# Second layer of the expert pairs with the tokens as columns, turned back by DMA, in a Mamba-2 and top-1 routing kernel

## The chip, the core and the metric

The kernel runs on one core of a Trainium2 chip. A core has engines that run their own instruction streams and wait for each other on semaphores: TensorE (PE, matrix multiplies, with weight loads PEld beside them), VectorE (DVE), ScalarE (ACT), GpSimd (POOL) and SyncE (SP, which issues DMA transfers here). The metric is the device time of one execution in microseconds (us), the median of several runs.

## What is computed

Two stages follow each other. The first is a state-space layer (chunks of a scan over 768 places, 4 batches, 8 heads of 32); it yields x, 3072 tokens of 256 numbers. The second, which the change concerns, sends each token to one of 8 experts:

```python
logits = x @ w_gate                      # 3072 x 8
expert_idx = np.argmax(logits, axis=1)
probs = np.exp(logits - logits.max(-1, keepdims=True))
probs /= probs.sum(-1, keepdims=True) + 1e-09
gate_w = probs[np.arange(N), expert_idx]
for e in range(E):                       # E = 8
    mask = expert_idx == e
    h = np.maximum(x[mask] @ w1[e], 0.0)         # 256 -> 1024
    out[mask] = gate_w[mask, None] * (h @ w2[e]) # 1024 -> 256
```

How many tokens an expert gets is known only while the kernel runs.

## The kernel before

**Places and passes.** Each expert has a stretch of rows in the DRAM buffer `x_hbm`; a token's row holds its 256 numbers, its 8 logits and its number. GpSimd's indirect DMAs scatter the tokens there (`place`, L553). A first pass handles the first 256 places (CA) of every expert, expert by expert; a second pass handles the next 192 places (CB), two experts at a time, as pairs v = 0 to 3; a general loop after that is for inputs with more tokens yet (L983). Rows with no token carry a number out of bounds, so that their output is dropped.

**One expert.** A tile `xs` holds rows with tokens as partitions. The first layer needs x with its 256 numbers as partitions: `halves` (L645) splits the fp32 words into 16-bit halves on VectorE (L651), a DMA transposes the 128x128 blocks (L653), and `words` (L657) joins the halves to `xT`. `m_h` (L692) runs the first layer: for each of the 8 blocks of 128 hidden units, two matmuls with a 128x128 block of w1 loaded and n columns of `xT` streaming, into one of four PSUM banks (`h_ps`, L681), then a relu on ScalarE into `hT` (L696), with hidden units as partitions and tokens as columns. `m_y` (L717) runs the second layer with 128 tokens of `hT` as the loaded side and the 256 columns of w2 streaming, so the result has tokens as partitions; `put` multiplies by the gate, a number per partition, and `send` (L708) scatters the rows to `out`. The profile shows every fp32 matmul as two records.

**The second pass** (L962 to L980). Of a pair, 128 places of each expert lie in `xs[:, 0]` and `xs[:, 1]`, the last 64 of each share a tile `xh`. The number of columns of `m_h` is chosen at run time: `over` (L567) makes for each pair a class from its greater expert's count, and `tc.Switch` (L966) jumps to one of five cases, with widths of 128, 144, 160, 176 and 192. Only TensorE and ScalarE enter the cases (`pairs_on`, L896); the other engines jump past. A case holds both experts' `m_h` and, from the second case on, `m_half` (L726): the second layer of the last 64 places of both experts, side by side in the array, scaled by the gate into `yh`. After the case come `send(yh)`, the hint that tells the sequencers of TensorE and ScalarE which case is next (`switch_hint`, L974), and for the next pair the joining of words (`b_words`), the gates (`b_gates`: VectorE and ScalarE's Exp) and the transpose of the pair after it (`next_halves`). The second layer of the 128 first places, `m_y` for both experts, stands last, after the switch (L979).

**Order.** All of it stands under `tc.manual_schedule()` (L779): each engine executes its own instructions in the order in which the program writes them. Where a tile name has n buffers (`bufs=n`), the n+1st tile of that name takes the first one's place and waits for its readers. `hT` has three buffers, `xT` three, `pl` and `plT` two each. Memsets on VectorE (L965) clear `hT` from column 144 on before each pair, for columns that a case does not write but `m_half` reads.

The transfers of the second pass are the pairs' rows (L606 and L609), the transposes, both on SyncE's queue, and the scatters on GpSimd's.

Of the kernel before, what the change touches and what calls it, by code (L numbers as in the profile page):

```python
# [9 lines left out]
FP32 = mybir.dt.float32  # L10
BF16 = mybir.dt.bfloat16
I32 = mybir.dt.int32
U16 = mybir.dt.uint16
AX = mybir.AxisListType.X
ALU = mybir.AluOpType
# [5 lines left out]
N, DM, E, F = 3072, 256, 8, 1024  # L21
# [14 lines left out]
CA, CB = 256, 192  # L36
CAP = CA + CB
TA = CA // 128
NK = -(-(N - CAP) // 128)
NR = N + 128  # L40
EW = 2


@with_exitstack
def ssd_then_moe(ctx, tc, x, ad_in, az_in, B, BT, CT, w_gate, w1, w2, out):
# [521 lines left out]
    def over(tb, pp):  # L567
        cp = pp.tile([128, RG + 1, E], FP32, name="cn", tag="rank", bufs=1)
        nc.tensor.matmul(cp[:, 0], lhsT=ones_bf, rhs=cnt[:, len(RGS) + 1, :], start=True, stop=True)
        cn = tb.tile([128, E], FP32, name="cn")  # L570
        nc.vector.tensor_tensor(out=cn, in0=cp[:, 0], in1=base2, op=ALU.add)
        nc.vector.tensor_tensor(out=cn, in0=cn, in1=base_f, op=ALU.subtract)
        ov = tb.tile([128, E], FP32, name="ov")
        nc.vector.tensor_scalar(out=ov, in0=cn, scalar1=float(127 - CAP), scalar2=0.0, op0=ALU.add, op1=ALU.max)
        nc.vector.tensor_copy(nk[:, 0:E], ov)
        nc.vector.tensor_scalar(out=nk[:, 0:E], in0=nk[:, 0:E], scalar1=7, scalar2=None, op0=ALU.logical_shift_right)
        fl = tb.tile([128, 2], FP32, name="fl")
        nc.vector.tensor_reduce(fl[:, 0:1], ov, axis=AX, op=ALU.max)
        nc.vector.tensor_scalar(out=nk[:, E:E + 1], in0=fl[:, 0:1], scalar1=127.0, scalar2=None, op0=ALU.is_gt)
        nc.vector.tensor_copy(nk[:, E + 1:2 * E + 1], cn)  # L580

        ml = tb.tile([128, E // 2], FP32, name="ml")
        nc.vector.tensor_reduce(ml, cn.rearrange("p (b i) -> p b i", i=2), axis=AX, op=ALU.max)
        nc.vector.tensor_scalar(out=ml, in0=ml, scalar1=float(15 - CA - 128), scalar2=0.0, op0=ALU.add, op1=ALU.max)
        nc.vector.tensor_scalar(out=ml, in0=ml, scalar1=64.0, scalar2=None, op0=ALU.min)
        cl = nk[:, 2 * E + 1:]
        nc.vector.tensor_copy(cl, ml)
        nc.vector.tensor_scalar(out=cl, in0=cl, scalar1=4, scalar2=None, op0=ALU.logical_shift_right)


    ex = [dict() for _ in range(E)]
# [28 lines left out]

    def gate_out(sub, n):
        nc.scalar.activation(sub, sub, func=ACT.Exp)
        gt = ea.tile([128, TA], FP32, name="gate", bufs=5)[:, 0:n]
        nc.vector.tensor_reduce(gt, sub, axis=AX, op=ALU.add)
        nc.vector.tensor_scalar(out=gt, in0=gt, scalar1=1e-9, scalar2=None, op0=ALU.add)
        nc.vector.reciprocal(gt, gt)
        return gt
# [5 lines left out]
        return p  # L633

    def new_xT():
        return ea.tile([128, KT, CA], FP32, name="xT", bufs=3)

    def a_xT(e, pp, tag):
        ex[e]["xT"] = new_xT()
# [49 lines left out]
    def new_hT(mo):  # L689
        return mo.tile([128, FT, CA], FP32, name="hT", bufs=3)  # L690

    def m_h(e, xT, hT, n, pp, between=None):  # L692
        for f in range(FT):

            p = up(xT[:, :, 0:n], w_sb[e][0], f, n, pp, 128 if e == f == 0 and n == CA else CA)
            nc.scalar.activation(hT[:, f, 0:n], p, func=ACT.Relu)  # L696
            if between and f == FT // 2:
                between()

    def put(p, xs, gt, mo, scalar=True, last=False):  # L700
        yo = mo.tile([128, DM], FP32, name="yo", bufs=3)
        if scalar:
            nc.scalar.mul(yo, p, gt)  # L703
        else:
            nc.vector.tensor_scalar(out=yo, in0=p, scalar1=gt, scalar2=None, op0=ALU.mult)  # L705
        send(yo, xs, last)
# [8 lines left out]
        tc.add_to_no_dep_group("sc", s_.ins)  # L715

    def m_y(e, hT, xs, gt, mo, pp, between=None, scalar=True, last=False):  # L717
        p = pp.tile([128, DM], FP32, name="y_ps", tag="y", bufs=2)
        for f in range(FT):
            nc.tensor.matmul(p, lhsT=hT[:, f], rhs=w_sb[e][1][:, f * DM:f * DM + DM], start=(f == 0),  # L720
                             stop=(f == FT - 1))
            if between and f == FT // 2:
                between()
        put(p, xs, gt, mo, scalar, last)

    def m_half(v, mo, pp):  # L726

        p = pp.tile([128, DM], FP32, name="yh_ps", tag="rank", bufs=1)
        for f in range(FT):
            for i in range(2):  # L730
                nc.tensor.matmul(p[64 * i:64 * i + 64, :], lhsT=pr[v]["hT"][i][:, f, 128:CB],  # L731
                                 rhs=w_sb[2 * v + i][1][:, f * DM:f * DM + DM], start=(f == 0), stop=(f == FT - 1))
        nc.scalar.mul(yh, p, pr[v]["gh"])  # L733
# [45 lines left out]
    with tc.manual_schedule():  # L779
# [118 lines left out]
        def ab(e, t):  # L898
            def then():

                if e >= 1 and late:
                    place(late.pop(0))
                if e == E - 1 and t == 0:
                    b_words(0)
                if 2 <= e < 2 + E // 2 and t == 1:
                    v = e - 2
                    r = nc.values_load(nk[0:1, 2 * E + 1 + v:2 * E + 2 + v], engines=pairs_on, min_val=0, max_val=4,
                                       skip_runtime_bounds_check_because="one of five classes")
                    cls.append({g: r for g in pairs_on})
            return then  # L910
        def b_gates(v):
            r = pr[v]
            r["gate"] = gate_out(gate_in(r["xs"], TA), TA)
            r["gh"] = gate_out(gate_in(r["xh"], 1), 1)
        for e in range(E + 1):
            def nxt():
                if e == 0:
                    ex[0]["sub"] = gate_in(ex[0]["xs"], TA)
                    empty(2)
                    empty(3)  # L920
                    a_load(2)
                    a_load(3)
                    load_w(2, (0,))
                if e == 1:
                    rank_pe(last, rank_ps)
                    rank(last)
                if e == 2:
                    over(tb, pp)
                if e + 1 < E:
                    a_words(e + 1)  # L930
                    ex[e + 1]["sub"] = gate_in(ex[e + 1]["xs"], TA)
                next_halves(e + 2)
                if 1 <= e and e + 2 < E:
                    load_w(e + 2)
                if e == 0:
                    load_w(1, (1,))
                    load_w(2, (1,))
                    empty(4)
                    empty(5)
                if e == 1:  # L940
                    empty(6)
                    empty(7)
            if e < E:
                ex[e]["hT"] = new_hT(mo)
                m_h(e, ex[e]["xT"], ex[e]["hT"], CA, pp, nxt)
                ex[e]["gate"] = gate_out(ex[e]["sub"], TA)
                if e == E - 1:
                    b_gates(0)
            if e == E:
                tc.switch_hint(cls[0], 5, "p0")  # L950
            if e > 0:
                for t in range(TA):
                    m_y(e - 1, ex[e - 1]["hT"][:, :, 128 * t:128 * t + 128], ex[e - 1]["xs"][:, t],
                        ex[e - 1]["gate"][:, t:t + 1], mo, pp, ab(e - 1, t), e < E)
                if e + 3 < E:
                    a_load(e + 3)
                elif e + 3 - E < E // 2:
                    b_load(e + 3 - E, mo)

        yh = mo.tile([128, DM], FP32, name="yh", bufs=1)  # L960
        nc.vector.memset(yh, 0.0)
        for v in range(E // 2):  # L962
            pr[v]["hT"] = [new_hT(mo) for _ in range(2)]
            for h in pr[v]["hT"]:
                nc.vector.memset(h[:, :, 144:CB], 0.0)  # L965
            for c in tc.Switch(cls[v], 5, f"p{v}"):  # L966
                for i in range(2):
                    m_h(2 * v + i, pr[v]["xT"][i], pr[v]["hT"][i], 128 + 16 * c, pp)
                if c:
                    m_half(v, mo, pp)  # L970

            send(yh, pr[v]["xh"][:, 0])
            if v + 1 < E // 2:
                tc.switch_hint(cls[v + 1], 5, f"p{v + 1}")  # L974
                b_words(v + 1)
                b_gates(v + 1)
                next_halves(E + v + 2)
            for i in range(2):
                m_y(2 * v + i, pr[v]["hT"][i][:, :, 0:128], pr[v]["xs"][:, i],  # L979
                    pr[v]["gate"][:, i:i + 1], mo, pp, None, False, (v, i) == (E // 2 - 1, 1))  # L980
        mo_.close()
    more = nc.values_load(nk[0:1, E:E + 1], min_val=0, max_val=1, skip_runtime_bounds_check_because="a truth value")
    with tc.If(more > 0):  # L983
# [49 lines left out]
```

## Time and profile before

| | |
|---|---|
| median of three runs | 271.99 us (271.18 to 272.0) |
| span in the profile | 270.0 us |
| granted TensorE clock | 0.992 of full speed |
| busy: PEld, DVE, ACT, POOL | 213.7, 110.7, 104.5, 87.0 us |
| second pass, first to last matmul | 194.56 to 262.8 us |
| first-layer records L685, all forms | 90.3 us in 516 records |
| second-layer records L720 | 84.9 us in 384 records |
| half tiles L731 | 7.3 us in 64 records |

A line of a group view names the source line, engine and operation, the tiles (output <- inputs), shapes and count, then busy time and mean length. [...] records start closer together than they are long, so the time that they take is read from the starts of the first and last. In timelines each line has start, length, what, and in brackets how long the engine was idle before it and what it waited for. Names ending in q are sequencers: branches and register moves, which count as no engine's busy time.

### The profile page before, as it was taken

What the parts mean: (1) busy time and instruction counts of PE and PEld (TensorE: products, weight loads), DVE (VectorE), ACT (ScalarE), POOL (GpSimd) and SP (SyncE); (2) the same over time, 40 slices, a digit from 0 to 9 for tenths busy, and PEclk for the clock granted to TensorE, in tenths of its full rate; (3) what the DMA queues carried; (4) which work ended last, traced back from release to release, by engine and by line L of the source; (5) the groups of instructions that cost most, each with busy time, mean ns of one, the idle gap of its engine ahead of it and who ended that gap; (6) DMA issues with size and microseconds to landing.
All of it is one profiled execution on the core that took longest, in us unless ns stands there. A gap on an engine that the chain in (4) does not pass through costs nothing.

```text
span 270.0 us, 7603 instructions
## 1 busy us (share of the span) xinstructions
PE 252.9 (94%) x3044; PEld 213.7 (79%) x3067; DVE 110.7 (41%) x358; ACT 104.5 (39%) x304; POOL 87.0 (32%) x171
## 2 busy tenths in 40 slices
PE   8799898999997999999999999999999999999990
PEld 2577677677776888888888888888998978989770
DVE  4889887888854240421211111233225115321010
ACT  6958574655543423223232323141050520604200
POOL 5666875866720002025504120202211102121021
PEclk9999999999999999999999999999999999999996
DMA  6956767671434899949695959533330601401010
GB/s 182 374 172 171 228 199 236 165 247 51 135 118 101 212 367 310 384 177 294 236 256 202 279 199 335 130 91 78 103 85 9 94 4 30 90 6 40 2 35 28
DMA packets 29715, 43.57 MB, mean 161 GB/s; under 512 B 16203, under 2 KB 19917, under 8 KB 27984
## 3 DMA queue, kind: packets, MB, share of 16 engines
q1 hardware_dynamic: 27152, 36.32, 45.4%
q0 software_dynamic: 2496, 6.41, 7.1%
q8 instruction: 36, 0.59, 0.9%
q14 instruction: 31, 0.25, 0.3%
HBM read 29.10 MB, written 10.73 MB: 147 GB/s over the span
## 4 chain that ended last, share of the span: by engine, by line
PE 82%; DVE 5%; DMA 4%; issue 4%; POOL 2%; ACT 1%; POOLq 0%; ACTq 0%; DVEq 0%
PE h_ps L685 33%; PE y_ps L720 30%; PE y L176 5%; PE rows_ps L176 4%; PE g L176 3%; PE A L176 3%; PE yh_ps L731 3%; DVE L L359 2%; DMA x_hbm<-rows,pos 1%; DMA xs<-x_hbm 1%; DMA az<-in_az_dram 1%; DMA ct<-in_CT_dram 1%; DVE M L386 1%; PE rank L176 1%; DVE S L431 1%
## 5 line engine op out<-in xcount | busy, mean ns | idle before, releaser
L685 PE MATMUL h_ps<-xT,w 128*128 128x256 f32 (+3 forms) x516 | 90.3, 334 | 0.6 <-ACT xT L641 0.5
L685 PEld LDWEIGHTS h_ps<-xT,w 128*128 128x128 f32 x516 | 81.3, 190 | 8.2 <-ACT xT L641 0.7
L720 PE MATMUL y_ps<-w,hT 128*128 128x256 f32 x384 | 84.9, 380 | 0.0
L720 PEld LDWEIGHTS y_ps<-w,hT 128*128 128x128 f32 x384 | 72.6, 190 | 10.5 <-issue 0.8
L696 ACT ACTIVATE hT<-h_ps 128x256 f32<-128x256 f32 (+3 forms) x128 | 43.3, 339 | 60.8 <-PE h_ps L685 53.1
L711 POOL DMA_INDIRECT out_dram<-yo,xs x24 | 23.7, 988 | 91.1 <-ACT yo L703 64.7
L553 POOL DMA_INDIRECT x_hbm<-rows,pos x24 | 24.4, 1015 | 20.6 <-DMA x_hbm<-zrows 13.3
L359 DVE TENSOR_TENSOR_SCAN L<-abc,ident 128x512 f32<-128x512 f32 x24 | 29.1, 1213 | 0.0
L651 DVE COPY pl<-xs 128x256 uint16<-128x256 uint16 x44 | 10.4, 298 | 43.8 <-DMA xs<-x_hbm 43.7
L658 DVE COPY xT<-plT 128x512 uint16<-128x512 uint16 (+1 forms) x30 | 10.6, 415 | 33.6 <-DMA plT<-pl 27.8
L703 ACT ACTIVATE yo<-y_ps,gate 128x256 f32<-128x256 f32 x14 | 6.6, 474 | 39.4 <-PE y_ps L720 24.5
L386 DVE TENSOR_TENSOR M<-g,L 128x512 f32<-128x512 f32 x24 | 16.5, 687 | 5.6 <-PE g L176 5.1
L176 PE MATMUL rows_ps<-turn,yT 128*128 128x136 f32 x96 | 15.4, 283 | 3.5 <-issue 2.7
L705 DVE TENSOR_SCALAR yo<-y_ps,gate 128x256 f32<-128x256 f32 x10 | 4.8, 482 | 29.3 <-PE y_ps L720 29.3
L176 PE MATMUL g<-ctm,bt 32*64 32x128 f32 x384 | 16.3, 280 | 0.5 <-ACT ctm L293 0.4
L176 PEld LDWEIGHTS rows_ps<-turn,yT 128*128 128x128 f32 x96 | 14.5, 192 | 1.3 <-issue 0.4
L711 POOL DMA_INDIRECT out_dram<-yh,xh x4 | 3.9, 978 | 35.7 <-ACT yh L733 23.9
L470 ACT COPY rows<-rows_ps 128x264 f32<-128x264 f32 x24 | 9.1, 380 | 13.5 <-PE rows_ps L176 10.9
L176 PE MATMUL y<-M,xn 64*32 64x64 f32 x768 | 12.9, 223 | 1.2 <-issue 1.2
L457 ACT COPY yT<-y 128x256 f32<-128x256 f32 x24 | 8.9, 372 | 12.2 <-PE y L176 10.2
L176 PEld LDWEIGHTS g<-ctm,bt 32*64 32x64 f32 x384 | 10.4, 131 | 3.2 <-ACT ctm L293 0.9
L366 POOL TENSOR_TENSOR bs<-bn,L 128x128 f32<-128x128 f32 x22 | 9.0, 410 | 11.1 <-DVE L L359 10.0
(132 smaller groups left out, 203.3 us busy)
## 6 DMA issues: line engine op xcount, KB each, us to landing
w<-in_w_dram SPq DMA_DIRECT2D x13, 1024.0 KB
x_hbm<-zrows SPq DMA_DIRECT2D x8, 463.8 KB
xn<-in_x_dram SPq DMA_DIRECT2D x12, 256.0 KB
w<-in_w_dram SPq DMA_DIRECT2D x12, 256.0 KB
xs<-x_hbm SPq DMA_DIRECT2D x8, 265.0 KB
ct<-in_CT_dram SPq DMA_DIRECT2D x6, 256.0 KB
bt<-in_BT_dram SPq DMA_DIRECT2D x6, 256.0 KB
bn<-in_B_dram SPq DMA_DIRECT2D x6, 256.0 KB
```

The costliest lines, as they stand in the source:

```text
L176: i = nc.tensor.matmul(out, lhsT=lhsT, rhs=rhs, **kw)
L359: nc.vector.tensor_tensor_scan(out=s["L"].rearrange("p h i -> p (h i)"), data0=s["abc"], data1=ident8.rearrange("p h i -> p (h i)"), initi ...
L366: nc.gpsimd.tensor_tensor(out=bs[n % 2], in0=gr[n // CG]["B"][:, n % CG].rearrange("p (h m) -> p h m", h=8), in1=bc(st[n]["L"][:, :, CH - ...
L386: nc.vector.tensor_tensor(out=s["M"].rearrange("p (s v u) i -> p s v (u i)", s=2, v=2), in0=s["g"][:, :, 0:256].rearrange("p v (s f) -> p ...
L470: nc.scalar.copy(out=rt[g][:, k - R0[g], 0:DM + E], in_=p)
L553: s_ = nc.gpsimd.indirect_dma_start(out=x_hbm[:, :], out_offset=bass.IndirectOffsetOnAxis(ap=pos[:, k:k + 1], axis=0), in_=rt[grp[k]][:, k ...
L651: nc.vector.tensor_copy(pl[:, i, :, t], f[:, :, HB * t:HB * t + 128])
L658: nc.vector.tensor_copy(xT.bitcast(U16).rearrange("p t (j c) -> p c t j", c=2), tt)
L685: nc.tensor.matmul(p[:, i:min(i + step, n)], lhsT=w[:, c:c + 128], rhs=xT[:, t, i:min(i + step, n)], start=(t == 0), stop=(t == KT - 1))
L696: nc.scalar.activation(hT[:, f, 0:n], p, func=ACT.Relu)
L711: s_ = nc.gpsimd.indirect_dma_start(out=out[:, :], out_offset=bass.IndirectOffsetOnAxis(ap=xs[:, TOK:TOK + 1].bitcast(I32), axis=0), in_=y ...
L720: nc.tensor.matmul(p, lhsT=hT[:, f], rhs=w_sb[e][1][:, f * DM:f * DM + DM], start=(f == 0), stop=(f == FT - 1))
```

## The change

For pairs 0 to 2 the second layer is computed with its tokens as columns. `m_yT` loads 128x128 blocks of w2 and streams as many columns of `hT` as the first layer has made, for both experts inside the switch's case; the result, with the 256 outputs as partitions, is copied by ScalarE to `yT`. After the case `turn_back` splits it into 16-bit halves, a DMA transposes them as it does for the inputs, and `put_back` joins the words, multiplies by the gates on VectorE and sends three tiles. The second layer then streams only as many columns as there are places, in place of 256 for each tile, and `m_half` is not needed. Since columns may now be any number, the classes are 8 places apart from 112 to 192: eleven cases. Pair 3 keeps the old second layer. The next pair's words are joined ahead of the switch, and the gates are made one pair earlier (pairs 0 and 1 both behind expert 7); `xT` and `yo` get four buffers and the gates eight. The memsets of `hT` remain for pair 3 alone, from column 112.

```diff
+NCL = 11
-        nc.vector.tensor_scalar(out=ml, in0=ml, scalar1=float(15 - CA - 128), scalar2=0.0, op0=ALU.add, op1=ALU.max)
-        nc.vector.tensor_scalar(out=ml, in0=ml, scalar1=64.0, scalar2=None, op0=ALU.min)
+        nc.vector.tensor_scalar(out=ml, in0=ml, scalar1=float(7 - CA - 112), scalar2=0.0, op0=ALU.add, op1=ALU.max)
+        nc.vector.tensor_scalar(out=ml, in0=ml, scalar1=float(8 * NCL - 8), scalar2=None, op0=ALU.min)
...
-        nc.vector.tensor_scalar(out=cl, in0=cl, scalar1=4, scalar2=None, op0=ALU.logical_shift_right)
+        nc.vector.tensor_scalar(out=cl, in0=cl, scalar1=3, scalar2=None, op0=ALU.logical_shift_right)
...
+    def m_yT(e, hT, yT, n, pp):
+        p = pp.tile([128, 512], FP32, name="y_ps", tag="y", bufs=2).rearrange("p (m i) -> p m i", m=KT)[:, :, 0:n]
+        for m in range(KT):
+            for f in range(FT):
+                c = f * DM + m * 128
+                nc.tensor.matmul(p[:, m], lhsT=w_sb[e][1][:, c:c + 128], rhs=hT[:, f, 0:n], start=(f == 0),
+                                 stop=(f == FT - 1), skip_group_check=True)
+        nc.scalar.copy(yT[:, :, 0:n], p)
+
+    def turn_back(yT):
+        pl = ea.tile([128, TA + 1, 2, KT, 128], U16, name="pl", bufs=2)
+        f = [t.bitcast(U16).rearrange("p m (j c) -> p c m j", c=2) for t in yT]
+        for i in range(2):
+            nc.vector.tensor_copy(pl[:, i], f[i][:, :, :, 0:128])
+            nc.vector.tensor_copy(pl[:, 2, :, :, 64 * i:64 * i + 64], f[i][:, :, :, 128:CB])
+        tt = ea.tile([128, TA + 1, 2, KT, 128], U16, name="plT", bufs=2)
+        nc.sync.dma_start_transpose(out=tt.rearrange("p i c t j -> p (i c t) j"),
+                                    in_=pl.rearrange("p i c t j -> p (i c t j)"))
+        return tt
+
+    def put_back(v, tt, mo):
+        r = pr[v]
+        for i, (gt, xs) in enumerate(((r["gate"][:, 0:1], r["xs"][:, 0]), (r["gate"][:, 1:2], r["xs"][:, 1]),
+                                      (r["gh"], r["xh"][:, 0]))):
+            yo = mo.tile([128, DM], FP32, name="yo", bufs=4)
+            nc.vector.tensor_copy(yo.bitcast(U16).rearrange("p (m j c) -> p c m j", c=2, m=KT), tt[:, i])
+            nc.vector.tensor_scalar(out=yo, in0=yo, scalar1=gt, scalar2=None, op0=ALU.mult)
+            send(yo, xs)
...
                 if e == E - 1:
                     b_gates(0)
+                    b_gates(1)
...
         for v in range(E // 2):
+            end = v == E // 2 - 1
             pr[v]["hT"] = [new_hT(mo) for _ in range(2)]
-            for h in pr[v]["hT"]:
-                nc.vector.memset(h[:, :, 144:CB], 0.0)
-            for c in tc.Switch(cls[v], 5, f"p{v}"):
+            if end:
+                for h in pr[v]["hT"]:
+                    nc.vector.memset(h[:, :, 112:CB], 0.0)
+            else:
+                b_words(v + 1)
+            for c in tc.Switch(cls[v], NCL, f"p{v}"):
+                n = 112 + 8 * c
                 for i in range(2):
-                    m_h(2 * v + i, pr[v]["xT"][i], pr[v]["hT"][i], 128 + 16 * c, pp)
-                if c:
+                    m_h(2 * v + i, pr[v]["xT"][i], pr[v]["hT"][i], n, pp)
+                if not end:
+                    for i in range(2):
+                        m_yT(2 * v + i, pr[v]["hT"][i], yTs[i], n, pp)
+                elif n > 128:
                     m_half(v, mo, pp)
-            send(yh, pr[v]["xh"][:, 0])
-            if v + 1 < E // 2:
-                tc.switch_hint(cls[v + 1], 5, f"p{v + 1}")
-                b_words(v + 1)
-                b_gates(v + 1)
+            if end:
+                send(yh, pr[v]["xh"][:, 0])
+                for i in range(2):
+                    m_y(2 * v + i, pr[v]["hT"][i][:, :, 0:128], pr[v]["xs"][:, i],
+                        pr[v]["gate"][:, i:i + 1], mo, pp, None, False, i == 1)
+            else:
+                tc.switch_hint(cls[v + 1], NCL, f"p{v + 1}")
+                if v + 2 < E // 2:
+                    b_gates(v + 2)
+                tt = turn_back(yTs)
                 next_halves(E + v + 2)
-            for i in range(2):
-                m_y(2 * v + i, pr[v]["hT"][i][:, :, 0:128], pr[v]["xs"][:, i],
-                    pr[v]["gate"][:, i:i + 1], mo, pp, None, False, (v, i) == (E // 2 - 1, 1))
+                put_back(v, tt, mo)
```

## The prediction

> **What bounds the kernel now.** I read the page's parts 1 and 4 first, then the chain in order of time for the second pass, then the Tensor groups by form, and last the sequencers' branch records with the Scalar and Vector timelines around each pair's boundary.
>
> ```profile
> PE 252.9 (94%) x3044; PEld 213.7 (79%) x3067; DVE 110.7 (41%) x358; ACT 104.5 (39%) x304; POOL 87.0 (32%) x171
> ```
>
> TensorE is busy nearly always, so what it is given to do, and every gap in it, sets the time. The chain of work that ended last (start, length, what) over the four pairs:
>
> ```profile
> 194.56 7.14 PE h_ps L685 x64
> 201.71 6.91 PE y_ps L720 x32
> 208.61 9.55 PE h_ps L685 x64
> 218.17 3.60 PE yh_ps L731 x32
> 221.77 7.10 PE y_ps L720 x32
> 228.88 7.14 PE h_ps L685 x64
> 236.02 6.91 PE y_ps L720 x32
> 242.93 0.17 issue
> 243.10 8.95 PE h_ps L685 x64
> ```
>
> The pieces abut: pair 0 takes 14.05 us, pair 1 20.26, pair 2 14.05, with one visible gap of 0.17. To see what hides behind them, look at the Tensor sequencer's branches (line 1028 stands for those that the switch makes) in the stretches 201 to 206, 225 to 227 and 236 to 245 us:
>
> ```profile
> L1028 PEldq COMPARE_BRANCH  x1: 3128/3128/3128, 205.1 to 205.1; - x1
> L1028 PEldq COMPARE_BRANCH  x1: 290/290/290, 225.1 to 225.1; - x1
> L1028 PEldq COMPARE_BRANCH  x1: 3775/3775/3775, 239.2 to 239.2; - x1
> ```
>
> The entries to pairs 1 and 3 (cases 3 and 2) take 3.1 and 3.8 us although their hints came 4.0 and 3.7 us earlier; the entry to pair 2 (case 0) takes 0.3. They cost nothing only because the sequencer is ahead of the array: at 239.17 it has sent everything up to 242.93, which is 3.76 us or 17 matmuls of 0.216. On ScalarE, timeline from 236 us:
>
> ```profile
> 236.06 0.28 ACT L696 ACTIVATE hT<-h_ps 128x128 f32<-128x128 f32 x1 [0.17 <-PE h_ps L685]
> 239.18 0.22 ACT L622 ACTIVATE gsub<-gsub 128x16 f32<-128x16 f32 x1 [2.85 <-issue]
> 240.36 0.21 ACT L622 ACTIVATE gsub<-gsub 128x8 f32<-128x8 f32 x1 [0.96 <-DVE gsub L618]
> 243.95 0.30 ACT L696 ACTIVATE hT<-h_ps 128x160 f32<-128x160 f32 x1 [3.39 <-PE h_ps L685]
> ```
>
> The 2.85 named "issue" and the 3.39 are not work: the records behind them are the branch out of pair 2's case at 236.06 with the next instruction at 238.75, and the branch into pair 3's case at 240.55 with the next at 243.27. From the last act in one pair's case to the first instruction in the next pair's, ScalarE takes 201.75 to 208.93 = 7.18 us, 221.85 to 226.60 = 4.75 (case 0), and 236.06 to 243.27 = 7.21. Today 6.9 to 7.2 us of second-layer matmuls that need no ScalarE lie just there. On VectorE, the same boundary:
>
> ```profile
> 207.52 0.49 DVE L651 COPY pl<-xh 128x256 uint16<-128x256 uint16 x2
> 209.16 0.79 DVE L965 MEMSET hT<- 128x384 f32 x2
> 213.04 0.65 DVE L658 COPY xT<-plT 128x512 uint16<-128x512 uint16 x2 [3.09 <-DMA plT<-pl]
> ```
>
> From the end of the last halves' copy (208.01) to the first use of the transposed words is 5.0 us; the next such pair of records, 227.82 to 233.43, gives 5.6.
>
> [...] ScalarE's exits cost 2.38 to 2.69 us, its entries to cases other than 0 cost 2.71. [...] I use the measured 17. [...] Measured starts of full 128-row records lie 216 ns apart at 256 columns, 149 at 176, 136 at 160: n/1.2 + 2.5. At 128 columns it is 112 instead of 109[...]. [...]
>
> **The change, part by part.** The reference's router counts make the greater expert of each pair 372, 418, 365 and 415 tokens, so the widths go from 128, 176, 128, 160 to 120, 168, 112, 160, and the cases from 0, 3, 0, 2 to 1, 7, 0, 6.
>
> Matmuls. Pair 1: the second layer becomes 64 records of 168 columns in place of the 3.60 and 7.10; a record at 168 is 142.5 ns, so 2 x 64 x 0.1425 = 18.24 against 20.26: -2.0. Pairs 0 and 2: 128 records each at 120 and 112 columns. By the line they would be 102.5 and 95.8 ns (13.1 and 12.3 us, -0.95 and -1.8); if the weight load holds 112 ns, 14.34 and 14.34, +0.3 each. No row shows a full fp32 load with fewer than 128 columns, so these are my two ends: -4.7 and -1.4 in sum. I take -1.4, since 128 already stands above the line.
>
> Second-layer output. Two Scalar copies a pair replace the yh scaling (0.47), about 0.35 each; only the last is exposed. Vector gains the turn's four copies (0.46 and 0.29 each, rows L658 and L651), a transpose of the same shape as the existing one, and three copies with three scalings for each of pairs 0 to 2. That is some 4 us of Vector a pair in a stretch where it is busy 4.4 of 14.2, and it is off the Tensor path except at pair 3. Memsets of hT for pairs 0 to 2 vanish (0.2 of wait). The gates moved ahead add two exps and their waits, 2.3 us on ScalarE, behind expert 7's relus; two y banks and 3.4 us of matmul a bank hide them. The xT words of the next pair are now made a pair early: for pair 2 about 17 us after pair 0's end, and pair 1 lasts over 18; for pair 3 about 16 us after pair 1's end, when pair 2 ends too. Hidden, the last barely. The entry to pair 0, now case 1, has 3.8 us of look-ahead: at most 0.3.
>
> The waits. This is what decides. The matmuls that used to lie between two switches now lie inside the first, so with E the end of a pair's last matmul, both engines leave one case and enter the next with nothing in between.
>
> TensorE: 17 records ahead is 1.8 to 2.4 us. Exit 0.3, hint and index arithmetic 0.9, entry 3.1 to 3.8: it resumes near E + 2 to E + 3. Behind the branch wait all first-layer matmuls; but four h banks (L681) then let only four groups go before a relu must free one.
>
> ScalarE: it leaves when its last yT copy starts, E + 0.08. Into pair 1: 7.18 more, 0.1 to the start, relu 0.31, 0.1 to TensorE: E + 7.8. Four groups of 4 x 0.1425 are 2.28, so TensorE is late by 5.5. Into pair 2 (case 0): 0.08 + 4.75 + 0.1 + 0.27 + 0.1 = 5.3, less 4 groups of 0.45 = 1.8: 3.5. Into pair 3 no gates stand between, 7.21 - 1.37 = 5.8, which would be 6.4 - 2.2 = 4.2; but here another wait is longer.
>
> VectorE into pair 3: its memset of hT[112:192] overlaps the 160 columns that the relus write (as in the 3.4 that ACT hT waits for DVE hT now), and it stands behind pair 2's put_back, which waits for the transposed result. E + 0.5 (copy and semaphore), two copies 0.7, transpose 5.3 (5.0 to 5.6), three copies and scalings of 0.46 + 0.29 = 2.25 (the scaling from SBUF between 0.27, a memset of that size, and 0.48, the PSUM row), memset of 640 elements 0.6 (0.27 at 256 and 0.38 at 384 extended), relu and semaphores 0.45: E + 9.8. Less 2.2 for four groups, less the 0.4 of gap and memset wait that pair 3 has already: 7.2.
>
> Sum: -1.4 + 5.5 + 3.5 + 7.2 = 14.8; 271.99 + 14.8 = 286.8, with 0.2 for pair 0's entry 287.0.
>
> **The rivals.** *The waits stay hidden*: hints would have to bring the cases in, and the memset not hold the relus. Then only matmuls count: 271.99 - 1.4 to -4.7 = 267.3 to 270.6, taken 269. For it: Tensor exits do hit, 0.3 each. Against it: every Scalar exit missed with a hint more than ten us old, and both entries to far cases missed on both engines. *Jumps alone*: the transposed result comes sooner, or the memset does not bind, and pair 3 waits for ScalarE: 4.2 - 0.4 in place of 7.2, with columns under 128 partly paid: 287 - 3.4 - 1.5 = 282. For it: 5.3 is the transpose of a busy stretch. Against: the program's order puts the memset last. *The clock falls too*: gaps of 5 to 7 us on TensorE, broken by 2 us of work, [...] two to three of them give 290.5 to 292. [...] Against: the burst of four groups inside each gap.
>
> **How the numbers follow.** The forecast 0.54, jumps alone 0.18, clock 0.21, hidden 0.07. The predicted time is 287.0. The range 280 to 292.5 holds the first three with the ends of the matmul pace (-3.3), the transpose (0.3) and the fetch (0.7 each); the hidden case is left out. Faster comes from the hidden case alone, less a share where one wait partly remains: 0.06 faster, 0.02 same, 0.92 slower.
>
> **What would show each step.** In the changed profile: records 142.5 ns apart in pair 1 and 112 in pairs 0 and 2; ScalarE idle some 7.2, 4.8 us between pairs; TensorE with four groups, then a wait on ACT hT, before pairs 1 and 2; ACT hT waiting on the memset before pair 3, near 9.5 us after pair 2's end. Wrong: Tensor gaps under 2 us at the boundaries, a memset that runs before put_back, or records under 105 ns. A PEclk well below 1 in the second pass would be the third rival.

## The result and the profile after

The changed kernel takes 297.54 us (median of four, 296.45 to 299.39) against 272.0 us: 1.0951 times as long, 95% interval 1.0879 to 1.1022. The profiled execution spans 294.7 us, 24.7 more than before. The forecast was slower, at 287.0; the time lies above the range. A run that lies over 1.5% above the fastest of its kernel, at a lower clock, is left out of the ratios in this document.

Part 1 and the clock row of part 2 of the page after:

```profile
PE 262.9 (89%) x3131; PEld 224.0 (76%) x3131; DVE 117.1 (40%) x378; ACT 105.8 (36%) x309; POOL 87.6 (30%) x171
PEclk9999999999999999999999999999869977966997
```

TensorE has more busy time and yet a smaller share, 89% for 94%: it stands still. And its granted clock, at full speed throughout the second pass before, drops three times. The matmuls in order of time, up to pair 3's first layer (start, length, what; in brackets the idle time ahead):

```profile
194.14 7.30 PE L686 MATMUL h_ps<-xT,w 128*128 128x120 f32 x64
201.28 7.31 PE L733 MATMUL y_ps<-hT,w 128*128 128x120 f32 x64
214.24 11.61 PE L686 MATMUL h_ps<-xT,w 128*128 128x168 f32 x64 [5.65 <-DVE pl L743]
225.68 9.28 PE L733 MATMUL y_ps<-hT,w 128*128 128x168 f32 x64
240.04 10.28 PE L686 MATMUL h_ps<-xT,w 128*128 128x120 f32 x64 [5.08 <-DVE gate L626]
250.16 7.31 PE L733 MATMUL y_ps<-hT,w 128*128 128x120 f32 x64
265.57 11.12 PE L686 MATMUL h_ps<-xT,w 128*128 128x160 f32 x64 [8.10 <-DVE yo L754]
```

The three gaps are 18.8 us in sum. The names in brackets are only the last events ahead of each start: VectorE's copies `pl` at 213.80, for instance, feed a transpose, not TensorE. What TensorE waits for is in its sequencer. The switch's branches, first those of the kernel before together, then those after in the stretches 204 to 215, 231 to 240 and 254 to 266 us (shortest, middle and longest in ns; of the two in each line after, the shorter and earlier one is the exit from a case, the other the entry to the next):

```profile
L1028 PEldq COMPARE_BRANCH  x7: 290/313/3775, 190.8 to 239.2; - x7
L1075 PEldq COMPARE_BRANCH  x2: 2351/3382/4412, 206.4 to 209.7; - x2
L1075 PEldq COMPARE_BRANCH  x2: 2496/3370/4244, 232.3 to 235.6; - x2
L1075 PEldq COMPARE_BRANCH  x2: 3708/4570/5431, 255.3 to 260.0; - x2
```

Before, every exit took 0.3 us and the slow entries 3.1 and 3.8. Now exits take 2.35, 2.50 and 3.71 and entries 4.41, 4.24 and 5.43, one behind the other. At the first boundary: exit at 206.44, 2.2 us ahead of the last matmul's end at 208.60; 2.35 + 0.88 of moves and hint + 4.41 lead to 214.1, and the first matmul starts at 214.24.

The lengths show the clock. At full clock and after a gap, 64 first-layer records take 9.38 us with 168 columns (e2_warm below), 7.38 with 128 (e1_y_in_case) and 8.95 with 160 (before); here those of pairs 1 to 3, with 168, 120 and 160, take 11.61, 10.28 and 11.12, together 7.3 more. The granted clock by stretch (the column after POOL's) says the same; before, it was 1.00 in every pair's stretch.

```profile
194.30:208.60 14.30, 14.29 (x129) 14.11 (x127) 2.92 (x10) 4.70 (x17) 0.98 (x1) 1.00 0.18 48
208.60:235.00 26.40, 20.73 (x128) 20.48 (x128) 7.09 (x30) 6.09 (x20) 3.13 (x3) 0.87 0.25 42
235.00:257.50 22.50, 17.42 (x128) 17.25 (x128) 7.48 (x30) 5.27 (x20) 3.14 (x3) 0.85 0.26 54
257.50:287.40 29.90, 21.83 (x128) 19.09 (x128) 4.54 (x11) 5.70 (x18) 4.90 (x5) 0.83 0.20 33
```

(Columns: length, busy time and instructions of PE, PEld, DVE, ACT and POOL, granted clock, DMA share, GB/s.) The clock records put the half-speed stretches (granted clock 0.50 in each) at 212.0 to 218.8, 239.3 to 246.1 and 259.8 to 270.0: they begin 3.4, 4.3 and 2.3 us into the gaps and reach over the matmuls behind them. 15.1 us of matmuls fall into them, and half of that, 7.5, is the loss again.

So the 24.7 us are: gaps +18.65 (0.17 was there before), clock +7.3, matmuls at full clock -1.05 (pair 0 +0.25, pair 1 -1.75, pair 2 +0.45, pair 3 none), and a start 0.25 earlier. By the distances of starts alone pairs 1 and 2 would be at -2.0 and +0.25; the rest is what a layer needs to start up after a gap.

ScalarE and VectorE at the boundaries, from the timelines after:

```profile
208.63 0.36 ACT L735 COPY yTb<-y_ps 128x240 f32<-128x240 f32 x1 [3.21 <-PE y_ps L733]
215.75 0.31 ACT L697 ACTIVATE hT<-h_ps 128x168 f32<-128x168 f32 x1 [2.77 <-PE h_ps L686]
241.93 0.47 ACT L697 ACTIVATE hT<-h_ps 128x120 f32<-128x120 f32 x2 [2.56 <-PE h_ps L686]
267.23 0.30 ACT L697 ACTIVATE hT<-h_ps 128x160 f32<-128x160 f32 x1 [9.32 <-DVE hT L1003]
```
```profile
258.28 0.29 DVE L743 COPY pl<-yTb 128x256 uint16<-128x256 uint16 x1
264.11 0.46 DVE L754 COPY yo<-plT 128x512 uint16<-128x512 uint16 x1 [5.54 <-DMA plT<-pl]
266.54 1.27 DVE L1003 MEMSET hT<- 128x640 f32 x2
```

The first relus come 7.15, 6.95 and 9.75 us after the last matmul of the pair before, the third waiting for the memset behind `put_back`; the first waits for its matmuls (PE h_ps), as ScalarE's sequencer was in the case at 215.4. That is near the chain that the prediction built on; but TensorE itself came 5.6, 5.1 and 8.1 us late and at half speed, so its four groups in the h banks were not finished when the relus began, and it never had to wait for them.

### The profile page after: what moved, and what is told of

The parts are those of the page before. It is cut to its first block, busy times and chain, and to the rows that moved or that the text cites. A ratio compares the mean times of both kernels' runs of the same rounds, so it can differ in the third digit from the quotient of the medians.

```text
span 294.7 us, 7785 instructions
## 1 busy us (share of the span) xinstructions
PE 262.9 (89%) x3131; PEld 224.0 (76%) x3131; DVE 117.1 (40%) x378; ACT 105.8 (36%) x309; POOL 87.6 (30%) x171
## 4 chain that ended last, share of the span: by engine, by line
PE 83%; issue 4%; DMA 4%; DVE 3%; POOL 2%; ACT 1%; POOLq 0%; ACTq 0%; DVEq 0%
PE h_ps L686 33%; PE y_ps L721 20%; PE y_ps L733 8%; PE y L177 6%; PE g L177 4%; PE A L177 3%; PE rows_ps L177 3%; PE abc L177 2%; PE wake_ps L177 2%; DMA plT<-pl 2%; DVE L L360 1%; DMA x_hbm<-rows,pos 1%; PE yh_ps L763 1%; DMA xs<-x_hbm 1%; PE rank L177 1%
## 5 line engine op out<-in xcount | busy, mean ns | idle before, releaser
L686 PE MATMUL h_ps<-xT,w 128*128 128x256 f32 (+4 forms) x516 | 97.2, 353 | 19.3 <-DVE yo L754 8.1
L686 PEld LDWEIGHTS h_ps<-xT,w 128*128 128x128 f32 x516 | 88.2, 208 | 26.6 <-DVE yo L754 8.3
L697 ACT ACTIVATE hT<-h_ps 128x256 f32<-128x256 f32 (+3 forms) x128 | 42.7, 337 | 70.6 <-PE h_ps L686 57.6
L721 PE MATMUL y_ps<-w,hT 128*128 128x256 f32 x288 | 63.6, 379 | 0.0
L721 PEld LDWEIGHTS y_ps<-w,hT 128*128 128x128 f32 x288 | 54.6, 190 | 7.8 <-PE yh_ps L763 0.4
L733 PE MATMUL y_ps<-hT,w 128*128 128x120 f32 (+1 forms) x192 | 23.9, 285 | 0.0
L733 PEld LDWEIGHTS y_ps<-hT,w 128*128 128x128 f32 x192 | 23.6, 191 | 0.0
L625 DVE TENSOR_REDUCE gate<-gsub 128x2 f32<-128x16 f32 (+1 forms) x16 | 2.6, 162 | 31.6 <-ACT gsub L623 31.6
L458 ACT COPY yT<-y 128x256 f32<-128x256 f32 x24 | 8.9, 373 | 12.3 <-PE y L177 10.2
L177 PEld LDWEIGHTS g<-ctm,bt 32*64 32x64 f32 x384 | 10.5, 131 | 3.5 <-ACT selx L132 0.8
```

Source lines behind the costliest of these rows:

```text
L177: i = nc.tensor.matmul(out, lhsT=lhsT, rhs=rhs, **kw)
L686: nc.tensor.matmul(p[:, i:min(i + step, n)], lhsT=w[:, c:c + 128], rhs=xT[:, t, i:min(i + step, n)], start=(t == 0), stop=(t == KT - 1))
L733: nc.tensor.matmul(p[:, m], lhsT=w_sb[e][1][:, c:c + 128], rhs=hT[:, f, 0:n], start=(f == 0), stop=(f == FT - 1), skip_group_check=True)
```

## The experiments

Two theories. **F**: TensorE waits for its own instructions. A case of pairs 0 to 2 now holds 259 of them by the records (128 weight loads, 128 matmuls, a hint, a wait, the branch), where the largest of the kernel before holds 196 and is left in 0.3 us, and no matmul stands between one case and the next to cover the fetch; that an exit gets slow beyond some size of the case is at this point an assumption; the clock that falls in the gaps adds its part. **R**, the prediction: ScalarE's way from case to case and VectorE's memset bind. The kernel before ran beside each group of experiments: 270.22 (e1 to e4), 271.44 (e5 to e7), 269.95 (e6_again, e8 to e10) and 272.7 us (e11).

**The place in the case alone.** The kernel before, with its old second layer moved into the case:

```diff
                 if c:
                     m_half(v, mo, pp)
+                for i in range(2):
+                    for f in range(FT):
+                        nc.tensor.matmul(py[i], lhsT=pr[v]["hT"][i][:, f, 0:128], rhs=w_sb[2 * v + i][1][:, f * DM:f * DM + DM],
+                                         start=(f == 0), stop=(f == FT - 1))
...
-                m_y(2 * v + i, pr[v]["hT"][i][:, :, 0:128], pr[v]["xs"][:, i],
-                    pr[v]["gate"][:, i:i + 1], mo, pp, None, False, (v, i) == (E // 2 - 1, 1))
+                put(py[i], pr[v]["xs"][:, i], pr[v]["gate"][:, i:i + 1], mo, False, (v, i) == (E // 2 - 1, 1))
```

> The kernel before with one edit: the second layer of the 128 first places (m_y) stands inside the case, behind m_h and m_half; nothing is transposed back, five cases of 16 as before. TensorE then meets two switches with nothing between, while ScalarE leaves its case 6.9 us before TensorE does. Theory F (the changed kernel waits for TensorE's own instruction fetch): the case of pairs 0 and 2 [...] its exit takes 0.3 us, that of pair 1 (with m_half) [...] its exit takes about 2.4; the entries take 3 to 4.5 us with only 3.5 us of look-ahead; gaps of 1 to 2 us before pairs 1 and 3, 2 to 4 before pair 2; 276 to 280 us. Theory R (my prediction: ScalarE's leaving and entering binds): ScalarE is early, so the gaps are under 0.7 us each and the time is 272 to 274.

273.75 us, 1.0116 (1.0033 to 1.02), which leaves open whether the rise reaches 2%. The branches of the first two boundaries, exit and entry:

```profile
L1032 PEldq COMPARE_BRANCH  x2: 303/2176/4049, 201.5 to 202.7; - x2
L1032 PEldq COMPARE_BRANCH  x2: 1890/2278/2667, 223.4 to 226.2; - x2
```

Pair 0's case (196 instructions) is left in 0.3 us; pair 1's, which with `m_half` has 260, in 1.9; pair 2's in 0.3 and pair 3's in 1.9. The gaps are 1.35, 1.68 and 1.65, with ScalarE out of its case seven us before TensorE; R alone would show under 0.7. So the branches go as F has it, but F's time does not: 276 to 280 was named, and 273.75 lies in the range of R; the gap before pair 2 was to be 2 to 4. The gaps stay small and the clock stays at 1.00; TensorE's sequencer reached the first exit 4.0 us ahead of the array (201.54 against 205.57), for 2.2 in the changed kernel.

**A smaller case.** First with half of the new second layer left out (outputs 128 to 255 of pairs 0 to 2 aren't computed), about 195 instructions, still eleven cases:

```diff
-        for m in range(KT):
+        for m in range(1):
...
-        nc.scalar.copy(yT[:, :, 0:n], p)
+        nc.scalar.copy(yT[:, 0:1, 0:n], p[:, 0:1])
```

> The changed kernel with half of the transposed second layer left out (outputs 128 to 255 of pairs 0 to 2 aren't computed): the case has about 195 Tensor instructions instead of about 262. The work is 11.7 us less at full clock. If [...] exits take 0.3 us instead of 2.4, 2.5 and 3.7, the gaps fall from 5.7, 5.1 and 8.1 to about 3.5, 3 and 5, and the time is 276 to 281. If exits miss because the eleven cases lie far from their end, they still take 2.4 or more, and the time is 285 to 287.

280.33 us in a single run; all three exits 0.31 to 0.33. Then with only the last four matmuls of each case left out (outputs 128 to 255 of the second expert are incomplete sums), 243 instructions:

```diff
+                if e % 2 and m and f > 3:
+                    continue
...
-                                 stop=(f == FT - 1), skip_group_check=True)
+                                 stop=(f == (3 if e % 2 and m else FT - 1)), skip_group_check=True)
```

> The changed kernel with four matmuls of each case of pairs 0 to 2 left out (the last four of the second expert's outputs 128 to 255, so that these are incomplete sums): 243 Tensor instructions in a case by the records instead of 259, work 1.0 us less. If [...] the exits take 0.3 us, the gaps on TensorE fall from 5.7, 5.1 to 5.8 and 7 to 8 towards 3, ScalarE's late entry and the memset then show as waits of TensorE for ACT hT, and the time is 286 to 290. If an exit gets slow for another reason (more cases, no work between the switches), it stays over 2 us and the time at 293 to 298.

286.05 us, 1.0443 (1.035 to 1.0537), for 1 us less of matmuls. The three boundaries' branches:

```profile
L1077 PEldq COMPARE_BRANCH  x2: 328/2208/4088, 205.4 to 206.6; - x2
L1077 PEldq COMPARE_BRANCH  x2: 306/2130/3954, 227.7 to 229.0; - x2
L1077 PEldq COMPARE_BRANCH  x2: 323/2242/4160, 249.3 to 250.6; - x2
```

The limit lies between 243 and 259 instructions; where between the two isn't shown. The trace also has the fetches themselves, as packets of 16,384 bytes on the queue q8, which the page lists as `instruction` (38 packets, 0.62 MB in the changed kernel). Here two follow TensorE's entry to pair 0's case (192.35 and 195.52 us), and the exit at 205.40 takes 0.33. In the changed kernel one follows (191.66), and the next starts at 206.31, with the exit at 206.44. All cases of the second pass go that way, in every profile: with at most 243 instructions a second fetch starts 3 to 6 us after the first, with 259 or 260 it starts from 1.0 us ahead of the exit to 1.4 behind it. So with the hint at the head of every case the exits were short in the small cases alone, and 16 instructions more cost 2 us or more at each of three exits.

Now the other engines come up:

```profile
233.09 2.03 PE L686 MATMUL h_ps<-xT,w 128*128 128x120 f32 x16 [2.66 <-issue]
237.94 7.25 PE L686 MATMUL h_ps<-xT,w 128*128 128x120 f32 x48 [2.81 <-ACT hT L697]
```

TensorE starts pair 2 after 2.66 us, sends exactly four groups (16 records), and then stands 2.81 us for ScalarE: R's mechanism, which the fetch had hidden. The other two boundaries have gaps of 3.29 and 3.43 us and then stops of 0.29 and 0.85.

**The number of cases.** The changed kernel with five cases 16 apart, from 128:

```diff
-NCL = 11
+NCL = 5
...
-                n = 112 + 8 * c
+                n = 128 + 16 * c
```

> The changed kernel with five cases 16 places apart from 128, as before; pairs 0 and 2 take case 0, pair 1 case 3 (176 columns), pair 3 case 2. If the number of cases or the distance to the case taken made the branches longer, entries fall from 4.4, 4.2, 5.4 us towards the 3.1 and 3.8 of the kernel before (and 0.3 into case 0), and the time falls by 3 to 6 us. If only the size of a case and the missing work between two switches matter, exits stay over 2 and entries at 4 or more, except perhaps into case 0, and the time stays within 2 us of 297.

296.24 us in a single run. Exits 3.5, 3.4 and 2.8 us, entries 4.0 to case 3, 2.7 to case 0 and 4.2 to case 2. The number of cases isn't the cause; nor is the distance from a case to the switch's end, as e11 has eleven cases and short exits. Only the way into case 0, 2.7 us, is shorter.

**The clock.** Ten matmuls that nobody reads, 4.3 us, behind each hint:

```diff
                 tc.switch_hint(cls[v + 1], NCL, f"p{v + 1}")
+                wp = pp.tile([128, DM], FP32, name="warm_ps", tag="rank", bufs=1)
+                for _ in range(10):
+                    nc.tensor.matmul(wp, lhsT=w_sb[0][0][:, 0:128], rhs=w_sb[0][0][:, 0:DM], start=True, stop=True)
```

> The changed kernel with ten fp32 matmuls of 256 columns, 4.3 us, that nobody reads, between one pair's switch and the next on TensorE. If the clock that is granted after each gap costs what the records say (matmuls of pairs 1 to 3 that are 8.1 us longer than at full clock), the clock stays at 1 and the time falls by 7 to 8 us to about 290, the added matmuls lying in the wait for the branch. If the slow records come from something else, or if the added matmuls push the branch back, the time stays at 297 or rises to 302.

288.31 us, 1.0673 (1.0602 to 1.0744), clock 1.00 in the whole second pass. The first boundary and the last:

```profile
208.53 4.58 PE L1025 MATMUL warm_ps<-w 128*128 128x256 f32 x20 [2.01 <-issue]
213.34 9.38 PE L686 MATMUL h_ps<-xT,w 128*128 128x168 f32 x64 [0.24 <-issue]
...
257.83 2.43 PE L686 MATMUL h_ps<-xT,w 128*128 128x160 f32 x16 [0.55 <-issue]
261.75 6.79 PE L686 MATMUL h_ps<-xT,w 128*128 128x160 f32 x48 [1.49 <-ACT hT L697]
```

Pair 1's first layer is back at 9.38 for 11.61. Against the changed kernel's 1.0951 and 1.0867 (below) the ratio falls by 0.019 to 0.028, 5 to 8 us. The pauses did not shrink: from the end of a pair to the next first layer it is 6.82, 5.04 and 5.86 us, with two stops of 0.29 and 1.49 behind that, 0.7 more in sum than the gaps of the changed kernel. So the gain is the clock's part, 7.3 us by the lengths.

**Work between the switches.** The new second layer behind the switch, at the fixed width of 192:

```diff
-                if not end:
-                    for i in range(2):
-                        m_yT(2 * v + i, pr[v]["hT"][i], yTs[i], n, pp)
-                elif n > 128:
+                if end and n > 128:
                     m_half(v, mo, pp)
...
                 tc.switch_hint(cls[v + 1], NCL, f"p{v + 1}")
+                for i in range(2):
+                    m_yT(2 * v + i, pr[v]["hT"][i], yTs[i], CB, pp)
...
+                clear(v + 1)
                 tt = turn_back(yTs)
```

> The changed kernel with its transposed second layer moved out of the case, behind the switch, at the fixed width of 192 columns; the turn by DMA, the gates and the sends stay, and the clearing of hT stands ahead of the turn, one pair early. 10.4 us of matmuls lie between two switches. Theory F: no gap over 0.5 us, clock at 1, and the time is the sum of the matmuls: 272 + 3.3 (pair 0) - 0.7 (pair 1) + 3.3 (pair 2) = 278 to 279. If the turning back itself (transposes, Vector's copies, the sends) costs time, it shows here as more than 280.

285.99 us, 1.0583 (1.0496 to 1.0671): a miss of 7 us. TensorE's branches behave as F says, exits 0.3 and no gap at any entry. But four groups later it stands:

```profile
214.55 8.79 PE L686 MATMUL h_ps<-xT,w 128*128 128x168 f32 x48 [2.52 <-ACT hT L697]
238.73 7.25 PE L686 MATMUL h_ps<-xT,w 128*128 128x120 f32 x48 [3.22 <-ACT hT L697]
259.65 6.79 PE L686 MATMUL h_ps<-xT,w 128*128 128x160 f32 x48 [1.09 <-ACT hT L697]
```

ScalarE copies `yT` at the very end of the second layer, then (except ahead of pair 3) makes two exps that wait for VectorE, then takes 2.5 to 2.7 us into its case. Waits of 0.93, 2.52, 3.22 and 1.09, and two half-speed stretches of 3.4 us, which cost 1.7 each, come to some 11 us, which covers it; the time is 15.8 above the kernel before beside it, where 6 to 7 were expected. So the form of the second layer puts a ScalarE copy where the old form had none, and that cost in both places in which it stood.

**The memset.** Pair 3's memsets ahead of pair 2's turn, once alone and again beside the changed kernel:

```diff
+                if v + 2 == E // 2:
+                    pr[v + 1]["hT"] = [new_hT(mo) for _ in range(2)]
+                    for h in pr[v + 1]["hT"]:
+                        nc.vector.memset(h[:, :, 112:CB], 0.0)
                 tt = turn_back(yTs)
```

> The changed kernel with the memsets of pair 3's hT ahead of pair 2's turn instead of behind its put_back. Theory R (my prediction): they release ScalarE 3 us earlier and the time falls by 3. Theory F: TensorE gets into pair 3's case only 8.1 us after pair 2's end, when the memset is nearly done, so the gap stays 8 us and the time within 0.7 us.

> The changed kernel unchanged, on the same chip and in the same rounds as the next ones, so that differences of a few us can be told: 296 to 299 us. If the exit from pair 2's case (3.71 us in its first profile, against 2.3 to 2.8 for every other miss of this kind) was chance, this profile shows it under 3.

> The changed kernel with pair 3's memsets ahead of pair 2's turn, now in rounds. If the memset behind put_back costs time behind the late Tensor entry, this stays 3 to 6 us below the changed kernel in the same rounds; if the one run of 291.6 came from a shorter fetch [...], the two agree within 2 us.

The single run gave 291.63. Beside it the changed kernel takes 293.75 us (293.12 to 294.43), 1.0867 (1.0801 to 1.0934). The one with early memsets has two runs to compare, 290.73 and 293.5 (two more took 296.6 and 296.83): too few to tell a gain of 2 us from none. The profiles say more. In the second one the gap before pair 3 is still 8.07. In the first it was 5.85, with a shorter exit (2.65) and entry (4.33) on TensorE; the same kernel shows 3.82 and 5.31 the second time, so that isn't the memset's doing. The changed kernel's exit of 3.71 was 3.44 in e9_changed_again. The packets part the slow exits in two: in those of 3.4 to 3.8 us the fetch starts 0.9 to 1.4 us after the branch, in those of 2.0 to 2.8 within 0.3 us of it, and in e1's two of 1.9 about 1 us ahead of it. What decides between them isn't shown. With the ten added matmuls as well:

> The ten added matmuls of e2_warm and the early memsets together. In e2_warm pair 3's first relu started with the memset, 1.3 us after ScalarE was in its case, and TensorE waited 1.5 us for it. So this should be 1 to 1.5 us below e2_warm: 287. If ScalarE's own entry (4.8 us there) binds next to it, it gains under 0.5.

It takes 288.25 (1.066, 1.058 to 1.074) against 288.31: no difference beyond the spread, and a miss. In its profile ScalarE entered 5.0 us after its branch, TensorE 5.2. The clock was not held up there: one stop of 1.9 us ahead of the added matmuls, and they ran at half speed, 6.26 us for 4.58 in e2_warm.

```profile
255.70 6.26 PE L1022 MATMUL warm_ps<-w 128*128 128x256 f32 x20 [1.91 <-issue]
```

**The transposes and the fetch.** Pair 2's result not transposed (VectorE reads the halves as they lie; pair 2's output is left untransposed):

```diff
+        if not turn:
+            return pl
         tt = ea.tile([128, TA + 1, 2, KT, 128], U16, name="plT", bufs=2)
...
+                tt = turn_back(yTs, v < 2)
```

> The changed kernel without the transpose of pair 2's result: Vector's put_back reads the halves as they are, so pair 2's output is left untransposed; everything else is as it was. If the transpose in flight (some 400 KB in 256-byte packets) delays the instruction fetches into pair 3's case, TensorE's entry falls from 5.4 to about 4.3 us and ScalarE's from 5.5 to about 2.6, the gap before pair 3 from 8.1 to 6 or 7, and the time by 1 to 4 us, clock included. If the fetches are slow for another reason, both entries stay over 5 us.

TensorE's last exit and entry:

```profile
L1077 PEldq COMPARE_BRANCH  x2: 2286/3137/3988, 252.1 to 255.2; - x2
```

ScalarE's entry is 2.94 for 5.54 (4.7 in e9_changed_again). The packets show the delay: on the queue q14, an `instruction` queue too, whose packets of 8,192 bytes stand at ScalarE's branches, those of the changed kernel's last entry (branch at 260.67) start at 262.96, and one takes 1.57 us; at its other entries they start 0.9 us after the branch and take 0.4. (The transposes' own packets: by the pages, q1 carries 4,704 packets and 1.18 MB more after the change than before, so each of the three has some 0.39 MB in packets of about 250 bytes.) In the nine profiles in which that transpose is issued ahead of ScalarE's last branch, the entry takes 3.8 to 5.5. TensorE's entry is 4.0 for 5.4 (4.8), but the nine profiles have it at 3.9 to 5.4, and its exit is shorter too (2.29 for 3.71 and 3.44); so the gap, 5.16 for 8.1 and 7.2, can't be put down to the transpose alone. The time, 292.74 us (290.04 to 294.02; 1.085, 1.0772 to 1.0927) beside 293.75, doesn't tell the two apart: what the transpose is worth in time stays open.

**A finer version of the kernel before.** Nine cases, 8 apart from 128, and memsets ahead of the last put:

```diff
-            for c in tc.Switch(cls[v], 5, f"p{v}"):
+            for c in tc.Switch(cls[v], 9, f"p{v}"):
...
-                    m_h(2 * v + i, pr[v]["xT"][i], pr[v]["hT"][i], 128 + 16 * c, pp)
+                    m_h(2 * v + i, pr[v]["xT"][i], pr[v]["hT"][i], 128 + 8 * c, pp)
```

> The kernel before with nine cases, 8 places apart from 128, and the memsets of the next pair's hT ahead of the last put of this pair. Pair 1 streams 168 columns for 176 (64 x 6.7 ns = -0.43 us), pair 3 no longer waits for the memset (-0.25): 271.3 if the entries stay hidden behind m_y, up to 272.5 if nine cases make them take 4.3 us instead of 3.1 and 3.8.

271.23 us beside 271.44, 0.9997 (0.9978 to 1.0015): the same. The expected 0.7 us lies just outside the interval, which ends at 0.6. In the profile pair 1's first layer is 9.38 us for 9.72, and pair 3's is 8.95 as before: there was no memset wait of 0.25 to save. No version here beats the kernel before.

## Why the prediction was right and wrong

**Right: slower, and where.** The boundaries between cases set the time. In the changed kernel no wait of TensorE for the transposed result is found.

**Right: the matmuls.** -1.4 was taken; by the distances of starts -1.5 came (+0.25, -2.0, +0.25), and starting up after gaps took back some 0.45. At 168 columns the records start 142 to 143 ns apart, where the line through the measured 216, 149 and 136 has 142.5; a record is some 163 ns longer than that distance at every width here (379 for 216 at 256 columns, 275 for 112 at 120). At 120 columns the starts lie 112 ns apart, as at 128, so something other than the columns holds the pace; that it is the weight load wasn't tested. The lower end of -4.7 is out.

**Right as a description, wrong as the bound: ScalarE and VectorE.** First relus were forecast 7.36 us after the end of pair 0, 5.0 after pair 1 and about 9.4 after pair 2; they came at 7.15, 6.95 and 9.75, the first of them held by TensorE and close by luck. The second missed because the case was wrong: second-pass places begin at the greater of 256 and an expert's count in the first part (`base2`, L549), which makes pair 2's last place 375 in place of 365, 120 columns and case 1 instead of case 0. With TensorE sooner these waits appear, at 2.52, 3.22 and 1.09 us in e4 and at 0.29, 2.81 and 0.85 in e11, for 5.5, 3.5 and 7.2 in the forecast; in the changed kernel they lie behind TensorE's own lateness.

**The step that failed: "Exit 0.3, hint and index arithmetic 0.9, entry 3.1 to 3.8: it resumes near E + 2 to E + 3."** It resumed at E + 5.6, 5.1 and 8.1. The exit was taken over from the kernel before, though with the second layer in it the case has 259 instructions, and the exits seen there are of cases of 196 at most. Here it took 2.35, 2.50 and 3.71; e1, e3 and e11 show exits of 0.3 up to 243 instructions, e1 one of 1.9 at 260. With short exits, in e11, TensorE resumes at E + 3.3, 2.7 and 3.4. The entry took 4.2 to 5.4; why longer than 3.1 to 3.8 isn't shown (the hint stood only 0.4 us ahead of it, and at pair 3 a transpose was in flight). The sum of gaps, 18.65, is near the 16.2 that was forecast for them by luck: another engine made them. Of the 10.5 us between 287.0 and 297.54, the gaps are 2.4 and the clock 7.3.

**The term left out: the clock.** It was a rival at 0.21, at 290.5 to 292; no profile from before the change shows what a gap costs in clock, so that price was an assumption. It came at every gap, with 2.2, 2.9 and 2.2. Half speed lasted 6.8, 6.8 and 10.2 us, and 3.4 after shorter stops: stops of 1.9 us (e10) and 2.5 (e4) brought it, while 1.7 (e1) and 2.0 (e2) brought none. How long a stop it takes can't be read from that; in pair 3's gap half speed began 2.3 us in. "Broken by 2 us of work" was no protection: the changed kernel's gaps weren't broken, and in e11 pair 2's was (2.66, 2.0 of work, 2.81) and the clock fell all the same (0.979 in that profile's mean, for 0.992 in the one of before).

## What to carry to other kernels

Work that depends on a run-time case needs other work behind it: count what stands between one switch and the next on every engine that enters it, and compare it with exit plus entry (here 5.2 to 5.4 us on TensorE where the exit is short and 7.6 to 10.1 where it isn't, and 4.8 to 8.7 on ScalarE), not with the saving. Count TensorE's instructions in a case before anything is moved in: here exits took 0.3 us up to 243 of them and 1.9 to 3.8 from 259 on. And where a gap on TensorE may reach 2 us, price the half-speed stretch behind it as well (2.2 to 2.9 us at each gap of 5.1 to 8.1 here).

## What the runs showed that had not been expected

- An exit hint holds for a case of 243 Tensor instructions (0.3 us) and not for one of 259 (2.0 to 3.8 in the profiles here).
- ScalarE leaves every case with a delay of 2.4 to 3.2 us in every profile here, though that exit too is hinted at the head of the case.
- With a transpose in flight ScalarE's entry to pair 3's case took 3.8 to 5.5 us in nine profiles, and 2.9 in the one without it.
- A matmul record of 120 columns gains nothing over one of 128: 112 ns from start to start in both.
- Filling TensorE's wait with 4.3 us of useless matmuls made a kernel 5 to 8 us faster; the pauses stayed as long, and the half-speed stretches went.
